# A fused long-convolution and MLP layer on one core: the planner's order replaced by a written-out order, PSUM buffers named one by one, some small steps free to move between VectorE and GpSimd

## The chip, the cores and the metric

One core of one Trainium2 chip. The metric is device time in microseconds (us) of one launch. The kernel before took 324.35, 325.56 and 326.74 us in three runs; the median is 325.56. Engines: PE = TensorE, DVE = VectorE, ACT = ScalarE, POOL = GpSimd, SP = SyncE, which here only issues DMAs.

## What is computed

The reference, cut to what matters (S = 2048 positions, D = 640 channels, F = 1728, all tensors bf16):

```python
mod = (silu(c) @ w_mod).reshape(1, 6, 1, 640)          # six vectors of 640: sa, ca, ga, sb, cb, gb
sa, ca, ga, sb, cb, gb = mod[:, 0], mod[:, 1], ...
h = layernorm(A_q) * (1 + ca) + sa
k_shift[s] = sum over t < 4 of k_pad[s + t] * shift_k[:, 3 - t]       # per channel
kv = k_shift * A_v
y  = irfft(rfft(kv padded to 4096) * rfft(ssm_k padded to 4096))[:2048] + kv * ssm_D
x  = A_q + ga * (h * y)
h  = layernorm(x) * (1 + cb) + sb
# the mixer on h:
m1 = gelu(layernorm(h) @ w1)              # its four channel groups are then shifted by +1, -1, +2, -2 positions
x1 = h + shifted(m1) @ w2
x  = x + gb * (x1 + gelu(layernorm(x1) @ w3) @ w4)
```

## The kernel before, in words

The convolution is a Fourier transform written as matmuls in two stages. `stage1` (PE line 472, 20 units of 4 matmuls) transforms 128-position blocks that DVE has transposed into place (`to_slots`, line 459) with the small table `F1bd`; `stage2` (PE line 490, 32 units of 4 matmuls) applies the table `Gs`. Both write PSUM, and `evac` (lines 271 to 277) copies each unit to SBUF, on ACT (line 274) or on DVE (line 276). The pair runs twice: first for the filter `ssm_k`, then for kv. Before the second time `k_shift` (PE line 523, 10 units of 8 matmuls with diagonal weights built by POOL at line 421) makes the shifted k and DVE multiplies it by v (line 528). The tables come from POOL index patterns, range reductions on DVE (lines 360/361) or on POOL (`angles_pool`, lines 374 to 376, three instructions of 512 elements each), sines on ACT, and DMAs that copy table halves (lines 419/420). Also ahead of the transform, POOL adds `ssm_D` to the first column of each of the five filter blocks (line 507), and the DVE transpose of the block comes after that.

The six modulation vectors (`mods`) are made in 12 halves. Each half loads 400 KB of `w_mod` into one of three buffers (SP, line 543), multiplies on PE (5 matmuls, line 549), and is added to or copied from PSUM.

`inverse1` (10 steps, lines 639 to 666) copies a spectrum with its two partition halves exchanged (two DMAs at line 645, one issued by SP and one by POOL, into four buffers in turn), makes two products on DVE (line 649), 32 matmuls on PE (lines 660/661) and two evictions on ACT. `inverse2` (6 steps, PE line 699, evictions on ACT) gives y. Then, in 8 groups of two 128-row tiles: `chain_a` (lines 751 to 765: DVE lines 756 and 759, ACT sum of squares line 748), `chain_b`, `chain_c`, each ended by `ln_finish` (lines 729 to 745: six tiny POOL instructions of 128x2 elements, in two halves 734 to 736 and 741 to 743); `turn` transposes the result (PE line 789 for groups 0 to 2, DMA transposes on SP line 782 for others); `mm_w1` (PE 836/846), `mm_w2` (PE 891, DVE 899), `mm_w3` (PE 924), `mm_w4` (PE 942/948, DVE 965/970/971, output DMAs 974). The last tile of all is ended by `last_tile` (lines 976 to 993): PE makes its two halves of 320 columns one after the other, and each half has its own two DVE instructions (986, 989) and output DMAs (992).

`ln1_stats` (lines 583 to 590: two BN_STATS and one BN_AGGR per tile) and `make_q` (lines 629 to 634: one normalization and two DVE products per tile) prepare layernorm(A_q).

What sets the order: every step is a task with an engine (or two to choose from), a modelled cost, and the regions that it reads and writes. `Planner.run` places the tasks by list scheduling over these costs. Ties go by RANK, a list with one number for each of the 1047 tasks. The instructions are issued in that order on each engine. PSUM is a ring of four buffers of two banks each, handed out in rotation: the fifth allocation waits until the first is empty.

## Time and profile before

| | us |
|---|---|
| median of the runs (lowest, highest) | 325.56 (324.35, 326.74) |
| span of the profiled execution, first to last instruction | 327.8 |
| PE busy | 278.0 (85%) |
| DVE busy | 218.0 (66%) |
| ACT busy | 199.7 (61%) |
| POOL busy | 122.7 (37%) |
| chain of waits that ends last: PE 56%, DVE 17%, POOL 8%, DMA 6%, ACT 5%, issue 5% | |

The profiled execution's own time is its span, 327.8 us; it lies 2.2 us above the median of the runs. Lines of the form "L649" name lines of the kernel. "Idle before, releaser" means that the engine stood still before that instruction, and what ended the wait. "PEclk" is TensorE's granted clock, 1.00 being the full 2.4 GHz and 0.50 being 1.2 GHz.

### The profile page before, as it was taken

Reading aid. Unit: us, or ns where it says so; the run is one execution under the profiler, and the core shown is the slowest. Engines: PE = TensorE matmul, PEld = TensorE weight load, DVE = VectorE, ACT = ScalarE, POOL = GpSimd, SP = SyncE. Lnnn points to the kernel's source line nnn. Section 1 sums busy time; section 2 is a strip of 40 time slices with the busy share of each in tenths; the row PEclk is TensorE's granted clock in tenths of the full one; section 3 lists DMA queues with packets and bytes.
Section 4 is the critical chain, followed back from the end, with each engine's and each line's share of the span. In section 5 each row is a group of like instructions: output and inputs, shape, how many; then the busy total and the mean of one; then the engine's idle time right before and its main releaser. Section 6 shows DMA issues by size and latency. Waiting matters only on the chain.

```text
span 327.8 us, 7133 instructions
## 1 busy us (share of the span) xinstructions
PE 278.0 (85%) x2816; PEld 205.8 (63%) x2816; DVE 218.0 (66%) x422; ACT 199.7 (61%) x314; POOL 122.7 (37%) x268
## 2 busy tenths in 40 slices
PE   0689998897958864376899899999999999999992
PEld 0455445664558762254588688788878688778761
DVE  6978999987989999879788899641140532440152
ACT  3586469787937867988888889546606245004300
POOL 8998600215062158656666567420200112000000
PEclk9979999999968995559899999999999999999998
DMA  6999999979676530094010130342310003210011
GB/s 235 225 240 204 225 244 206 219 206 255 160 190 174 125 102 9 15 338 196 3 29 14 21 81 20 73 92 40 18 44 22 20 23 61 48 36 20 0 43 40
DMA packets 56690, 35.39 MB, mean 108 GB/s; under 512 B 38528, under 2 KB 53504, under 8 KB 56656
## 3 DMA queue, kind: packets, MB, share of 16 engines
q1 hardware_dynamic: 55248, 30.63, 39.6%
q0 software_dynamic: 1312, 4.26, 5.0%
q8 instruction: 22, 0.36, 0.5%
q14 instruction: 12, 0.10, 0.1%
q10 hardware_dynamic: 96, 0.04, 0.1%
HBM read 16.31 MB, written 2.62 MB: 58 GB/s over the span
## 4 chain that ended last, share of the span: by engine, by line
PE 56%; DVE 17%; POOL 8%; DMA 6%; ACT 5%; issue 5%; SPq 0%; DVEq 0%; POOLq 0%; ACTq 0%
PE ps_w L924 16%; PE ps_w L942 14%; PE ps_ksh L523 6%; PE ps_w L891 5%; PE ps_w L836 5%; DVE R L276 4%; DVE Rb L649 4%; DMA RH<-in_w_mod_dram 3%; PE ps_s L472 3%; ACT RG L748 2%; DVE ln_st L588 2%; POOL lnv L742 2%; DMA RK<-in_w_mod_dram 2%; PE ps_s L490 2%; PE ps_mod L549 1%
## 5 line engine op out<-in xcount | busy, mean ns | idle before, releaser
L924 PE MATMUL ps_w<-R,T 128*128 128x256 bf16 x560 | 63.6, 273 | 0.0
L924 PEld LDWEIGHTS <-T 128*128 128x128 bf16 x560 | 54.8, 98 | 6.9
L942 PE MATMUL ps_w<-T,R 128*128 128x320 bf16 x416 | 59.0, 299 | 0.0
L928 ACT ACTIVATE R<-ps_w 128x1024 bf16<-128x1024 f32 (+1 forms) x32 | 29.3, 915 | 42.5 <-PE ps_w L924 42.2
L942 PEld LDWEIGHTS <-R 128*128 128x128 bf16 x416 | 40.2, 98 | 16.5 <-issue 1.6
L965 DVE TENSOR_TENSOR T<-ps_w,R 128x640 bf16<-128x640 f32 x15 | 12.4, 824 | 53.7 <-PE ps_w L948 43.4
L274 ACT CAST T<-ps_s 128x1024 bf16<-128x1024 f32 x32 | 30.9, 1024 | 13.2 <-PE ps_s L472 13.1
L472 PE MATMUL ps_s<-F1bd,Rb 128*128 128x256 bf16 x160 | 22.7, 293 | 11.6 <-DVE Rb L459 10.1
L748 ACT ACTIVATE RG<-R 128x640 bf16<-128x640 bf16 x32 | 23.6, 736 | 14.1 <-DVE R L899 14.0
L274 ACT CAST R<-ps_s 128x640 bf16<-128x640 f32 x42 | 27.5, 734 | 4.0 <-PE ps_s L490 3.8
L891 PE MATMUL ps_w<-RG,R 128*128 128x320 bf16 x160 | 25.6, 312 | 3.8 <-ACT R L852 2.3
L472 PEld LDWEIGHTS <-Rb 128*128 128x128 bf16 x160 | 16.8, 106 | 16.9 <-DVE Rb L459 10.2
L660 PE MATMUL ps_i<-EA,Rb 128*128 128x128 bf16 x160 | 21.6, 236 | 5.3 <-DVE Rb L649 5.3
L274 ACT CAST T<-ps_i 128x1024 bf16<-128x1024 f32 x20 | 19.4, 1015 | 9.1 <-issue 4.7
L490 PE MATMUL ps_s<-T,RG 64*128 64x320 bf16 x256 | 23.1, 297 | 1.7 <-ACT R L274 1.0
L899 DVE SCALAR_TENSOR_TENSOR R<-ps_w,R 128x640 bf16<-128x640 f32 x16 | 13.1, 821 | 15.7 <-PE ps_w L891 15.7
L734 POOL TENSOR_SCALAR lnv<-stat 128x2 f32<-128x2 f32 x24 | 6.5, 272 | 45.2 <-DVE R L899 37.1
L891 PEld LDWEIGHTS <-R 128*128 128x128 bf16 x160 | 15.8, 102 | 11.4 <-ACT R L852 3.0
L836 PE MATMUL ps_w<-R,RG 128*128 128x256 bf16 x160 | 20.9, 291 | 2.1 <-DVE R L797 2.0
L661 PE MATMUL ps_i<-EB,Rb 128*128 128x128 bf16 x160 | 21.6, 236 | 0.8 <-DVE Rb L649 0.8
L742 POOL TENSOR_TENSOR lnv<-lnv,mhalf 128x2 f32<-128x2 f32 x24 | 20.5, 856 | 1.9
L660 PEld LDWEIGHTS <-Rb 128*128 128x128 bf16 x160 | 17.0, 107 | 6.3 <-DVE Rb L649 6.3
(151 smaller groups left out, 517.5 us busy)
## 6 DMA issues: line engine op xcount, KB each, us to landing
RH<-in_w_mod_dram SPq DMA_DIRECT2D x8, 400.0 KB, 5.2
Ra<-in_A_ssm_k_dram SPq DMA_DIRECT2D x5, 512.0 KB, 5.8
Ra<-in_A_q_dram SPq DMA_DIRECT2D x8, 320.0 KB, 9.1
out_dram<-RH SPq DMA_DIRECT2D x60, 40.0 KB, 1.6
T<-in_B_w_dram SPq DMA_DIRECT2D x1, 2160.0 KB, 13.4
T<-in_B_w_dram SPq DMA_DIRECT2D x1, 2080.0 KB, 10.0
RK<-in_w_mod_dram SPq DMA_DIRECT2D x4, 400.0 KB, 6.5
RK<-R POOLq DMA_DIRECT2D x5, 256.0 KB, 4.0
```

Of the source, the lines that this page charges most:

```text
L274: nc.scalar.copy(dst, src(ps.tile))
L472: nc.tensor.matmul(psv[:, ml, :], lhsT=xL[:, s0:s0 + P], rhs=F1r, start=True, stop=True)
L490: nc.tensor.matmul(psv[:, g], lhsT=Gs[p, k, 64 - 64 * cc:192 - 64 * cc], rhs=T1b[p, cc * 32 + k], start=(cc == 0), stop=(cc == 1), tile_po ...
L660: nc.tensor.matmul(psv[:, w, :], lhsT=Av[:, r_, :, g_], rhs=EAf, start=True, stop=False)
L661: nc.tensor.matmul(psv[:, w, :], lhsT=Bv[:, r_, :, g_], rhs=EBf, start=False, stop=True)
L742: nc.gpsimd.tensor_tensor(rs, rs, mhalf[:, 0:n], ALU.pow)
L748: add("ACT", 0.74, lambda e: nc.scalar.activation(junk, src, ACT.Square, scale=float(D) ** -0.5, accum_out=stat[:, li, 1, t:t + 1]), r=[sk ...
L836: nc.tensor.matmul(pt[:, fb, :], lhsT=w1_sb[:, b, 160 * fb:160 * fb + P], rhs=hT[:, b, :], start=(b == 0), stop=(b == ND - 1))
L891: nc.tensor.matmul(pt[:, hf, 0:320], lhsT=gsf[:, fb, c0:c0 + P], rhs=w2_sb[:, fb, 320 * hf:320 * hf + 320], start=(fb == 0), stop=(fb == 4))
L924: nc.tensor.matmul(pt[:, fl, :], lhsT=w3_sb[:, b, fb * P:(fb + 1) * P], rhs=xT[:, b, :], start=(b == 0), stop=(b == ND - 1))
L928: nc.scalar.activation(g3[g % 2][:, f0:f0 + fn, :], ps.tile[:, 0:fn, :], ACT.Gelu_apprx_tanh)
L942: nc.tensor.matmul(pts[i][:, hf, 0:320], lhsT=gg[:, fb, i * P:(i + 1) * P], rhs=w4_sb[:, fb, 320 * hf:320 * hf + 320], start=(fb == 0 and ...
```

## The change

RANK and the list scheduling are gone. ORDER is a written list of all 1055 tasks; a word such as `90P:0` says "task 90, on PE, in PSUM buffer 0". There are four PSUM buffers as before, but each has its own tag, so a task takes the buffer that the word names and not the next in rotation. Tasks that may run on two engines have the engine in the word too.

Of the steps that the change lets run on POOL or DVE, ORDER leaves all 12 pieces of `angles_pool` and the table E on POOL, and moves to DVE one of the two negations of `Gs`, one of the five `ssm_D` additions and 12 of the 24 first halves of `ln_finish`. Of the 20 `inverse1` evictions the last two go to DVE; the 12 of `inverse2` stay on ACT. In the last `mm_w4` the two column halves of the last tile lie in two PSUM buffers, not one.

```diff
-RANK = """
-6 8 9 11 12 13 14 15 17 18 19 21 22 24 25 26 27 29 381 86 103 20 16 49 638 369 93 684 23 109 168 254 105 161 91 81 540 69 391 68 60 28 378 34 373 71
...
+ORDER = """
+19G 0S 18D 20D 21G 23D 22D 24A 56G 27G 29D 28D 25A 2S 31A 30A 36G 37G 68G 69D 26G 90P:0 91A 86P:1 6S 87A 88P:2 89A 4S 72G 73D 104P:3 105A 102P:0
...
     def run(self):
-        engs = ("PE", "ACT", "DVE", "POOL", "SP")
...
+        order, seen = [], set()
+        for word in ORDER.split():
+            head, _, places = word.partition(":")
+            t = self.tasks[int(head[:-1])]
+            t.on = self.CODE[head[-1]]
+            for sl, place in zip(t.alloc, places):
+                sl.place = place
...
-    psA = ctx.enter_context(tc.tile_pool(name="psA", bufs=4, space=PSUM))
+    psA = ctx.enter_context(tc.tile_pool(name="psA", bufs=1, space=PSUM))
...
-            ps.tile = psA.tile(shape or [P, 2, 512], dt, name=name, tag="q2")
+            ps.tile = psA.tile(shape or [P, 2, 512], dt, name=name, tag="q" + ps.place)
...
-                nc.gpsimd.tensor_scalar(xs, ti, s_col, off, ALU.mult, ALU.add)
-                nc.gpsimd.tensor_scalar(xr, xs, MAGIC, MAGIC, ALU.add, ALU.subtract)
-                nc.gpsimd.tensor_tensor(xs, xs, xr, ALU.subtract)
...
+            add(both, {...}, lambda e, off=off: eng_of[e].tensor_scalar(xs, ti, s_col, off, ALU.mult, ALU.add), ...)
+            add(both, {...}, lambda e: eng_of[e].tensor_scalar(xr, xs, MAGIC, MAGIC, ALU.add, ALU.subtract), ...)
+            add(both, {...}, lambda e: eng_of[e].tensor_tensor(xs, xs, xr, ALU.subtract), ...)
...
     for b in range(ND):
-        add("POOL", 0.25, lambda e, b=b: nc.gpsimd.tensor_tensor(sT[:, b, 0:1], sT[:, b, 0:1], Dcol[:, b:b + 1], ALU.add),
+        add(("POOL", "DVE"), {...}, lambda e, b=b: eng_of[e].tensor_tensor(sT[:, b, 0:1], sT[:, b, 0:1], Dcol[:, b:b + 1], ALU.add),
...
     def ln_finish(li, t0, n):
         def f(e):
-            nc.gpsimd.tensor_scalar(nm, s1, -1.0 / D, None, ALU.mult)
-            nc.gpsimd.tensor_tensor(rs, nm, nm, ALU.mult)
-            nc.gpsimd.tensor_scalar(rs, rs, -1.0, EPS, ALU.mult, ALU.add)
+            eng_of[e].tensor_scalar(nm, s1, -1.0 / D, None, ALU.mult)
+            eng_of[e].tensor_tensor(rs, nm, nm, ALU.mult)
+            eng_of[e].tensor_scalar(rs, rs, -1.0, EPS, ALU.mult, ALU.add)
...
     def mm_w4(g):
-        pss = (Slot(), Slot())
+        pss = tuple(Slot() for _ in range(3 if g == 7 else 2))
...
+                tl = [pst(s, name="ps_w4") for s in pss] if i == 0 else [s.tile for s in pss]
+                pts = [[tl[0], tl[0]], [tl[1], tl[-1]]]
...
-            t1 = add("DVE", 0.48, lambda e, c=c, hf=hf: nc.vector.tensor_tensor(bo[:, c], ps.tile[:, hf, 0:320], gbv[:, c], ALU.mult),
+            t1 = add("DVE", 0.48, lambda e, c=c, hf=hf: nc.vector.tensor_tensor(bo[:, c], pss[hf].tile[:, hf, 0:320], gbv[:, c], ALU.mult),
```

POOL at the start of the program. Before (the `ssm_D` additions are line 507, Ra holds the filter blocks, R_67 is scratch for table angles, F1bd is the table of `stage1`):

```order
L374 TENSOR_SCALAR R_67<-R_67,s64t,offc 128x512
L375 TENSOR_SCALAR R_67<-R_67 128x512
L376 TENSOR_TENSOR R_67<-R_67 128x512
L507 TENSOR_TENSOR Ra<-Ra,Dcol 128x1 x3
L398 AFFINE_SELECT F1bd<-F1c 128x256
L399 AFFINE_SELECT F1bd<-F1bd 128x256
L507 TENSOR_TENSOR Ra<-Ra,Dcol 128x1
L374 TENSOR_SCALAR R_67<-R_67,s64t,offc 128x512
```

After (the same steps are lines 307, 309, 311 for the angles, 440 for the additions, 333/334 for F1bd):

```order
L307 TENSOR_SCALAR R_67<-R_67,s64t,offc 128x512
L440 TENSOR_TENSOR Ra<-Ra,Dcol 128x1
L333 AFFINE_SELECT F1bd<-F1c 128x256
L334 AFFINE_SELECT F1bd<-F1bd 128x256
L440 TENSOR_TENSOR Ra<-Ra,Dcol 128x1
L309 TENSOR_SCALAR R_67<-R_67 128x512
L311 TENSOR_TENSOR R_67<-R_67 128x512
L440 TENSOR_TENSOR Ra<-Ra,Dcol 128x1
```

The first addition and the `stage1` table now stand ahead of two of the three angle instructions; before, they stood behind all three.

SP, the loads of the front. Before (line 301 is a DMA transpose of a k or v block, 576 a quarter of half of A_q, 543 a half of a modulation weight, 645 an `inverse1` copy; above these rows stand eight more transposes):

```order
L301 DMA_TRANSPOSE R_68<-in_A_k_dram 128x2048
L301 DMA_TRANSPOSE R_68<-in_A_v_dram 128x2048
L576 DMA Ra<-in_A_q_dram 32x8x640 x4
L543 DMA RK<-in_w_mod_dram 128x5x320
L543 DMA RH<-in_w_mod_dram 128x5x320
L576 DMA Ra<-in_A_q_dram 32x8x640 x4
L543 DMA RH<-in_w_mod_dram 128x5x320 x2
L645 DMA RG<-R_67 64x2048
L543 DMA RH<-in_w_mod_dram 128x5x320
L543 DMA RK<-in_w_mod_dram 128x5x320
```

After (lines 234, 509, 476 for these; 354 and 355 are the table copies, all six of which POOL issued before; above these rows stand three transposes, of k, v and k):

```order
L234 DMA_TRANSPOSE R_68<-in_A_v_dram 128x2048
L354 DMA RG<-RG 64x1536
L225 DMA c_col<-in_c_dram 128x5x1
L509 DMA Ra<-in_A_q_dram 32x8x640
L354 DMA RG<-RG 64x1536 x2
L355 DMA RG<-RG 64x1536
L476 DMA RH<-in_w_mod_dram 128x5x320
L355 DMA RG<-RG 64x1536
L509 DMA Ra<-in_A_q_dram 32x8x640 x3
L476 DMA RH<-in_w_mod_dram 128x5x320
L234 DMA_TRANSPOSE R_68<-in_A_k_dram 128x2048
```

The table copies, half of A_q and the first two modulation loads now stand between the second and the third pair of k and v transposes.

DVE where `inverse1` ends and `chain_a` begins. Before (649 is an `inverse1` product, 588/589 are `ln1_stats`, 756/759 `chain_a`, 633/634 and 626 `make_q`; six more pairs of 588/589 stand between the first two rows):

```order
L649 TENSOR_TENSOR Rb<-R_68,R_67 128x4x8x64
...
L588 BN_STATS ln_st<-Ra 128x6 x2
L589 BN_AGGR mv_96<-ln_st 128x2
L756 TENSOR_TENSOR R_68<-Rb,RQ 128x8x5x16 x2
L759 SCALAR_TENSOR_TENSOR Ra,stat<-R_68,Ra 128x640 x2
L633 TENSOR_TENSOR RQ<-RQ,modv 128x640
```

After (582 the product, 210 an eviction from PSUM, 566/567 `make_q`, 521/522 `ln1_stats`; two more pairs of 521/522 stand between the last two rows):

```order
L582 TENSOR_TENSOR Rb<-R_68,RK 128x4x8x64
L210 CAST T_66<-ps_i_1463 128x128x8
L210 CAST T_66<-ps_i_1486 128x128x8
L567 TENSOR_TENSOR RQ<-RQ,modv 128x640 x2
L566 TENSOR_TENSOR RQ<-RQ,modv 128x640
L567 TENSOR_TENSOR RQ<-RQ,modv 128x640
L521 BN_STATS ln_st<-Ra 128x6 x2
L522 BN_AGGR mv_96<-ln_st 128x2
...
L689 TENSOR_TENSOR R_68<-Rb,RQ 128x8x5x16
```

Between the last product and `chain_a` stand three `ln1_stats` where there were seven, and two evictions and four `make_q` products that stood elsewhere. Before the first product, DVE now has two `make_q` normalizations, two products of line 633, five of line 634 and one `stage1` eviction less than before, and one negation and one addition more; three of the `make_q` products stand between the first `inverse1` products.

Three more moves are told in words. On PE, 7 of the 10 `k_shift` units stood ahead of the filter's `stage2` and 3 among its first units; now 4 stand ahead of it and 6 among the `stage1` units of kv. Of the 12 modulation units 11 stood behind the filter's `stage2` and ahead of kv's, and one after 3 of its 32 units; now 2 stand at the end of the filter's `stage2`, 4 among kv's `stage1`, and 6 are spread over kv's `stage2`, the last one behind its last unit. Of the 10 pairs of `inverse1` copies four stood ahead of the first product before, and one does after; the last three quarters of the second half of A_q are loaded after the copies. And the first `mm_w4` stands later in PE's order: behind 6 tiles of `mm_w2` and 120 matmuls of `mm_w3`, where it stood behind 4 tiles and 70.

## Rows read from the trace of the kernel before

**Rows 1.** By stretch: length, busy PE, PEld, DVE, ACT, POOL, PEclk, DMA share, GB/s
```profile
8.00:92.00 84.00, 72.32 (x556) 42.82 (x556) 75.17 (x101) 62.82 (x86) 37.35 (x58) 0.98 0.98 215
...
123.00:142.00 19.00, 7.83 (x371) 4.83 (x351) 17.34 (x46) 17.33 (x31) 14.06 (x31) 0.52 0.18 50
142.00:190.00 48.00, 42.25 (x327) 31.80 (x328) 39.62 (x100) 40.06 (x79) 28.75 (x68) 0.90 0.28 90
190.00:322.00 132.00, 131.50 (x1092) 103.79 (x1092) 50.58 (x107) 56.00 (x93) 23.22 (x70) 1.00 0.19 40
```
**Rows 2.** Timeline of PE (start us, length, instructions; idle before and its releaser)
```profile
10.07 5.03 PE L472 MATMUL ps_s<-F1bd,Rb 128*128 128x256 bf16 x24 [10.07 <-DVE Rb L459]
...
142.14 4.43 PE L836 MATMUL ps_w<-R,RG 128*128 128x256 bf16 x20 [1.26 <-DVE R L797]
...
154.87 3.89 PE L891 MATMUL ps_w<-RG,R 128*128 128x320 bf16 x16 [2.28 <-ACT R L852]
...
160.09 2.36 PE L836 MATMUL ps_w<-R,RG 128*128 128x256 bf16 x20 [0.77 <-DVE R L797]
...
317.79 3.71 PE L942 MATMUL ps_w<-T,R 128*128 128x320 bf16 x26
```
**Rows 3.** Timeline of DVE, six places
```profile
7.96 10.02 DVE L459 STREAM_TRANSPOSE Rb<-Ra 128x1024 int32<-128x1024 int32 x5 [1.44 <-POOL Ra L507]
...
91.61 1.21 DVE L649 TENSOR_TENSOR Rb<-R,RG 128x2048 bf16<-128x2048 bf16 x1
...
116.55 0.87 DVE L588 BATCH_NORM_STATS2 ln_st<-Ra 128x6 f32<-128x320 bf16 x2
...
123.55 0.84 DVE L756 TENSOR_TENSOR R<-Rb,RQ 128x640 bf16<-128x640 bf16 x2
...
321.53 0.49 DVE L986 TENSOR_TENSOR T<-ps_w,modv 128x320 bf16<-128x320 f32 x1 [1.76 <-PE ps_w L942]
...
322.30 0.48 DVE L986 TENSOR_TENSOR T<-ps_w,modv 128x320 bf16<-128x320 f32 x1
```
**Rows 4.** Timeline of POOL: the start, and the first ln_finish
```profile
6.32 1.31 POOL L376 TENSOR_TENSOR R<-R 128x512 f32<-128x512 f32 x1
7.60 0.33 POOL L507 TENSOR_TENSOR Ra<-Ra,Dcol 128x1 bf16<-128x1 bf16 x2
...
127.09 0.43 POOL L734 TENSOR_SCALAR lnv<-stat 128x2 f32<-128x2 f32 x1
...
128.47 0.32 POOL L741 TENSOR_TENSOR lnv<-stat,lnv 128x2 f32<-128x2 f32 x1
...
130.31 0.22 POOL L734 TENSOR_SCALAR lnv<-stat 128x2 f32<-128x2 f32 x1
```
**Rows 5.** The chain of waits, 57 to 79 us (start us, us, what)
```profile
57.35 5.48 DMA RH<-in_w_mod_dram
...
63.76 5.01 DMA RH<-in_w_mod_dram
...
73.24 5.69 DMA RK<-in_w_mod_dram
```
**Rows 6.** DVE groups by line (count, busy us, mean ns, idle before)
```profile
L276 DVE CAST T<-ps_s 128x1024 bf16<-128x1024 f32 x8 | 9.4, 1211 | 0.4 <-PE ps_s L472 0.4
...
L633 DVE TENSOR_TENSOR RQ<-RQ,modv 128x640 bf16<-128x640 bf16 x16 | 7.7, 483 | 0.0
L346 DVE TENSOR_SCALAR offc<-offc 128x1 f32<-128x1 f32 x1 | 0.1, 143 | 0.0
```
**Rows 7.** DMA issues, 91 to 118 us (KB each, median us to landing)
```profile
RK<-R POOLq DMA_DIRECT2D x3, 256.0 KB, 4.2
```
**Rows 8.** Timeline of SP (an issue's length includes its wait)
```profile
34.90 3.12 SPq L301 DMA_TRANSPOSE R<-in_A_v_dram  x1
...
47.62 10.11 SPq L543 DMA_DIRECT2D RH<-in_w_mod_dram  x2
...
323.70 1.82 SPq L992 DMA_DIRECT2D out_dram<-RH  x4
```

More of the change, by code (lines that the diff above doesn't have):

```diff
@@ L55 @@
+1001S 1028P:2 1029A 1030P:0 985D 989S 926S 1024P:1 1031A 987S 1010P:32 986S 988S 979D 983S 980S 1026P:0 925S 927S 1012D 1025A 928S 1013D 1016S 1011P
+1018D 982S 1014S 981S 1019D 1021S 1020S 1023S 1027A 1032P:130 1022S 1035D 1036D 1017S 1015S 1040S 1037S 1033P 1043D 1039S 1044D 1048S 1047S 1038S
+1045S 1034P 1049D 1050D 1053S 1052A 1046S 1051S 1054A
 """
 class Task:
-    __slots__ = ("no", "eng", "cost", "fn", "deps", "prio", "lat", "alloc", "frees", "left", "succ", "start", "end", "on", "ready", "kb", "rate", "port")
+    __slots__ = ("no", "eng", "cost", "fn", "deps", "lat", "alloc", "frees", "succ", "on", "kb", "rate", "port", "act")
@@ L123, in run @@
     def run(self):
-        engs = ("PE", "ACT", "DVE", "POOL", "SP")
-        free = dict.fromkeys(engs, 0.0)
-        ready = {e: [] for e in engs}
-        slots = []
-        order = []
-        wire = 0.0
-        held = {"DVE": 0.0, "POOL": 0.0}
-        rank = RANK.split()
-        if rank:
-            for t in self.tasks:
-                t.prio = (int(rank[t.no]), t.no)
-        def cost(t, e):
-            return t.cost[e] if isinstance(t.cost, dict) else t.cost
-        def push(t):
-            for e in (t.eng if isinstance(t.eng, tuple) else (t.eng,)):
-                ready[e].append(t)
@@ L218 @@
     small = ctx.enter_context(tc.tile_pool(name="small", bufs=2))
-    psA = ctx.enter_context(tc.tile_pool(name="psA", bufs=4, space=PSUM))
+    psA = ctx.enter_context(tc.tile_pool(name="psA", bufs=1, space=PSUM))
     pl = Planner(4)
     add = pl.add
-    eng_of = {"ACT": nc.scalar, "DVE": nc.vector}
+    eng_of = {"ACT": nc.scalar, "DVE": nc.vector, "POOL": nc.gpsimd}
     Ra = mem.tile([P, 10240], BF, name="Ra")
@@ L266, in cd, with dma, evac @@
         return 0.14 + 0.00104 * n
-    def dma(eng, kb, fn, r=(), w=(), prio=None, rate=330.0):
-        return add(eng, {"SP": 0.5, "POOL": 0.6}, lambda e: fn(nc.sync if e == "SP" else nc.gpsimd), r, w, prio, kb=kb, rate=rate)
-    def evac(dst, src, n, ps, w, prio=None, eng=("ACT", "DVE")):
+    def dma(eng, kb, fn, r=(), w=(), rate=330.0):
+        return add(eng, {"SP": 0.5, "POOL": 0.6}, lambda e: fn(nc.sync if e == "SP" else nc.gpsimd), r, w, kb=kb, rate=rate)
+    def evac(dst, src, n, ps, w, eng=("ACT", "DVE")):
         def f(e):
@@ L1004 @@
            lambda q: q.dma_start(w4_sb[64:128, NF - 1, :], B_w4[(NF - 1) * P:F, :])]
[L1005 to L1006 removed]
+    dma("SP", 2200, w3t[0], w=[("T01", 0, ND * FP)])
+    dma("SP", 2200, w3t[1], w=[("T01", 10240, 10240 + NF * D, "w4")])
     for i in (2, 3):
[L1008 removed]
+        dma("SP", 100, w3t[i], w=[("T01", 10240, 10240 + NF * D, "w4")])
     def f(e):
         nc.gpsimd.tensor_copy(w3_sb[:, :, F:FP], w3_sb[:, :, F - 64:F])
[L1012 removed]
+    add("POOL", 0.6, f, w=[("T01", 0, ND * FP)])
     made = 5
     for g in range(8):
[L1015 to L1018 removed]
+        ra = chain_a(g)
+        rb = chain_b(g, ra)
+        chain_c(g, rb)
         while made < NT and made <= 2 * g + 6:
[L1020 removed]
+            make_q(made)
             made += 1
[L1022 removed]
+        mm_w1(g)
         if g >= 1:
[L1024 removed]
+            mm_w2(g - 1)
         if g >= 2:
[L1026 to L1028 removed]
+            mm_w3(g - 2)
+            mm_w4(g - 2)
+    mm_w2(7)
     for g in (6, 7):
[L1030 to L1031 removed]
+        mm_w3(g)
+        mm_w4(g)
     order = pl.run()
[L1034 to L1038 removed]
     with tc.manual_schedule():
```

461 lines of the change are left out of this document (207 added, 254 removed), and 27 rows, old and new, of the table RANK.

## The prediction

> **What bounds the kernel now.** I read the busy time by stretch first, because one share for the whole run hides that the kernel has two halves. From 190 to 322 us PE is busy for 131.50 of 132 us at full clock [rows 1]: nothing that only reorders can shorten that part, and the matmuls are the same in number. Everything that can be won lies before 190 us and after 322. From 8 to 92 us PE is busy for 72.32 of 84, ACT for 62.82, but DVE for 75.17: DVE is the nearest to a bound, with 8.83 us idle. From 123 to 142 us PE works for 7.83 of 19 us at a granted clock of 0.52 while DVE and ACT each work for 17.3: this is the chain of small layernorm steps that feeds the first `mm_w1`. From 142 to 190 PE is busy for 42.25 of 48, 5.75 idle.
>
> Then the timelines, for the events that each stretch hands on. DVE starts its first transpose at 7.96 us after 1.44 us of waiting for POOL [rows 3], and PE's first matmul waits for DVE until 10.07 [rows 2]. The first `inverse1` product starts at 91.61, the seven `ln1_stats` behind the last product at 116.55, `chain_a` at 123.55 [rows 3], the first `mm_w1` at 142.14 [rows 2]. PE ends at 317.79 + 3.71 = 321.50, and DVE's last steps only then begin [rows 2, 3]; the span ends at 327.8. So the forecast is a sum of how much earlier each of these events comes.
>
> **The change part by part.** All terms are made against the profiled span, 327.8 us.
>
> *Start.* POOL reaches the first `ssm_D` addition at 7.60 because an angle instruction stands ahead of it until 6.32 + 1.31 = 7.63 [rows 4]. The addition now stands two angle instructions earlier, so the wait of 1.44 us goes [rows 3]; DVE is busy with its own angles until 6.5, and that is late next. Gain 1.4. Least 0.8, if the first filter block lands later than the addition could run.
>
> *Front, from there to the first product.* Three things. (a) DVE work that now stands behind the first product: two normalizations and two products of `make_q` and five more of its products, nine instructions at about 0.48, and one `stage1` eviction at 1.21 [rows 6], 5.5 us; one negation and one addition come in, about 0.5 (I price them by the 128x640 product, 0.48, from above and by the tiny 0.143 from below [rows 6]). Net 5.0. (b) Of DVE's 8.83 us of idle [rows 1], 1.44 is counted under the start; 7.4 is left. The chain of waits shows what much of it hangs on: three loads of a modulation weight, 5.48, 5.01 and 5.69 us [rows 5], stand one behind the other in the chain between 57 and 79, because the matmul of one half frees the buffer for a later load and all these matmuls stand together. The new order spreads the twelve halves from the filter's `stage2` to the end of kv's, so a load of 5.5 us has other PE work over it. Nothing in the rows says that all idle goes; I take half, 3.7, with the ends at 0 and 7.4. (c) Against it, three `make_q` products now stand between the `inverse1` products: 3 x 0.48 = 1.4. Together 5.0 + 3.7 - 1.4 = 7.3.
>
> *Between the products and `chain_a`.* Seven `ln1_stats` filled 123.55 - 116.55 = 7.0 us, 1.0 each [rows 3]. Now two evictions at 1.21, four products at 0.48 and three `ln1_stats` stand there: 2.4 + 1.9 + 3.0 = 7.3. Loss 0.3. The evictions may move out of ACT's way the end of the last one, but `chain_a` is behind them on DVE either way; ends -1 and +1. The four `ln1_stats` that left go to the stretches behind, 4 us of DVE work beside matmuls.
>
> *`chain_a` to the first `mm_w1`*: 142.14 - 123.55 = 18.6 us [rows 2, 3], of which DVE and ACT each fill over 90% [rows 1]. The first half of an `ln_finish` took POOL from 127.09 to 128.47, 1.4 us with three instructions [rows 4]; on DVE three tiny instructions cost at least 3 x 0.143 = 0.43 [rows 6], I take 0.5. Two such steps stand in series ahead of the first `mm_w1`, so 2 x 0.9 = 1.8, and 0.7 more for `make_q` work that no longer stands in the chain's way. Gain 2.5; ends 0.6 (the second half waits for ACT's sum of squares anyway) and 4. The twelve moved halves are 12 x 0.5 = 6 us more for DVE; it had 48 - 39.62 = 8.4 idle between 142 and 190 and 81 after [rows 1], which covers them.
>
> The Trainium skill bears on this term ("Perfetto Trace Analysis", section "Optimizing Scalar/DVE Operations"): GpSimd and DVE share an SBUF read port, so moving work between these two might not help. The trace fits it in so far as the same tiny instruction took POOL 0.43 us at 127.09 and 0.22 at 130.31 [rows 4]; whether the port did that, no row shows. By that rule alone the term would be its lower end, 0.6, and the sum 1.9 us later, still inside the forecast's range.
>
> *First `mm_w1` to saturation.* PE loses 5.75 us of idle here, and 4.43 - 2.36 = 2.1 us by the half clock of the first `mm_w1` [rows 1, 2]. The largest single wait, 2.28 us for ACT before an `mm_w2` [rows 2], stands in the new order behind a second and a third `mm_w1`. I take 2.0, with ends -2 (DVE has 6 us of new halves and 4 of `ln1_stats` here) and +4.
>
> *End.* Both halves of the last tile were one PSUM tile, and DVE's first multiplication waited until 321.53 though half of the 26 matmuls were done at about 317.79 + 3.71 / 2 = 319.65 [rows 2, 3]. With two buffers the second half's multiplication is the one that waits, and starts at 321.53 instead of 322.30: 0.77. SP's last four output issues took 1.82 us [rows 8], and the two of the first half now go out before PE ends: 0.9 more. Gain 1.7; ends 0.8 and 1.9.
>
> Naming buffers freely, without a rotation, costs no instruction; where it removes a wait, that is part of the terms above.
>
> **Sum**: 1.4 + 7.3 - 0.3 + 2.5 + 2.0 + 1.7 = 14.6 us; 327.8 - 14.6 = 313.2 us for a profiled execution. The profile lay 2.2 above the median of the runs, so 311.0 us in the runs, 4.5% less than 325.56.
>
> **The rivals.**
>
> *The front gives nothing.* SP waits inside an issue: two modulation loads took SP 10.11 us at 47.62, because the second waited for its buffer [rows 8], and everything behind stood still. In the new order table copies, which need POOL's and ACT's tables, stand on SP ahead of six of the ten k and v transposes, which feed `k_shift` and so DVE. If they hold SP until 30 us (my assumption, a quarter into the front; no row shows the new wait), six transposes of 3.1 us end near 49, where the last ended at 38.0 before [rows 8], and kv is late. For it: POOL, which makes these tables, was busy for 37.35 us between 8 and 92 [rows 1]. Against it: before, the modulation loads that stand among kv's `stage1` were waited for only from 57.35 on [rows 5], so 49 need not be late. If it holds, 7.3 becomes 0 and the sum is 7.3 us: 318.3 in the runs.
> The Trainium skill states the same of the issuing side ("DMA: Bandwidth & Descriptors", section "Anatomy of one DMA — SWDGE (gpsimd) path"): a DMA's semaphore wait happens on the issuing sequencer before dispatch. The row of 10.11 us agrees.
>
> *No change to speak of.* PE's clock. From 123 to 142 it was granted 0.52 after sparse work [rows 1], and the first `mm_w1` ran at 4.43 instead of 2.36 [rows 2]. If the new order leaves such gaps that the next matmuls stay at half clock as well, each 10 us of full-clock work take 10 more; with that, the 2.0 lost and the front at half its gain the sum is 14.6 - 10 - 2.0 - 3.6 = -1.0: 326.6 in the runs. For it: the half clock stands in the row. Against it: the clock came back by 160 with the gaps that it had [rows 2].
>
> *Slower: `inverse1` starves on its copies.* Before, four of ten pairs of copies had been issued ahead of the first product; now one. A pair is 2 x 256 KB, POOL's half lands 4.2 us after its issue [rows 7], and the ten steps took (116.55 - 91.61) / 10 = 2.5 us each [rows 3]. It starts to decide once a pair takes more than 2.5 us. At 215 GB/s, the rate of the front [rows 1], a pair needs 2.4 us of wire, and with four buffers in turn three pairs can be under way: nothing is lost. If each waits instead until the step before has freed its buffer, nine steps take 4.2 each: 9 x 1.7 = 15 us. The three quarters of A_q behind the copies on SP, and the `ln1_stats` that read them, then come late as well, by some 4 us. 327.8 - 14.6 + 19 = 332.2, 330.0 in the runs. Against it: four buffers.
>
> **How the numbers follow.** A measurement of this kernel can tell a change of about 1% (3.3 us) from none. Forecast 0.62; the front gives nothing 0.20; no change to speak of 0.11; starving 0.07. Faster by over 1% are the first two and a little less of each, 0.81; within 1% 0.11; slower 0.08. The ends of the terms: if all gains are at their upper ends, 1.4 + 10.9 + 0.7 + 4 + 4 + 1.9 = 23 us, 302.7; not all will be, so the low end is 304.5. At the high side the range reaches over the first rival to 321.5; the second and the third lie outside.
>
> **What would show it.** Right: the first DVE transpose before 7 us; no modulation load of 5 us in the chain between 57 and 79; the first product at 83 to 86; `chain_a` at about 115; the first `mm_w1` at about 130; PE full for the same 131 us; the last but one multiplication of 128x320 starting about 2 us before PE ends. Wrong: a first product later than 90, waits of DVE on copies between products, a granted clock at 0.5 beyond 20 us after the first `mm_w1`, or SP standing in a table copy beyond 30 us.

## The result, and the profile after

The changed kernel took 314.55 us (median of four runs, 312.59 to 315.64). The kernel before had a fourth run, of 333.17 us, which counts as one of the chip's slow state and is left out, so its median stays 325.56 us. The ratio is 0.965, with a 95% interval of 0.958 to 0.972. That is 3.5% faster. The forecast was 311.0 us, 4.5% faster; the time lies inside the range.

The profiled execution of after spans 311.9 us, 15.9 less than the 327.8 of before, while the medians of the runs differ by 11.0. The two profiles overstate the gain by some 5 us. The run that the profile of after shows took 313.61 us, so a run is 1.7 us longer than its span. By that, the profiled execution of before belongs to a run of about 329.5, 3.9 above its median, and that of after lies 0.9 below its own. The terms below are told between these two profiles.

Windows of the kernel before, cut at its first DVE transpose, first product and `chain_a` (columns as in [rows 1]):

```profile
7.96:91.61 83.65, 72.32 (x556) 42.82 (x556) 74.81 (x100) 62.86 (x86) 37.13 (x57) 0.98 0.98 216
91.61:123.55 31.94, 24.68 (x548) 23.10 (x551) 29.64 (x43) 20.65 (x22) 13.12 (x29) 0.89 0.56 150
```

The same stretches after, then 57 to 82 and the stretches that answer to the rest of [rows 1]:

```profile
6.26:79.80 73.54, 68.87 (x556) 41.98 (x556) 70.98 (x93) 62.97 (x88) 35.70 (x54) 1.00 1.00 224
79.80:111.73 31.93, 24.34 (x471) 22.27 (x473) 31.06 (x39) 20.15 (x23) 8.24 (x15) 0.89 0.86 212
...
57.00:82.00 25.00, 22.21 (x214) 13.55 (x211) 23.79 (x37) 21.71 (x32) 6.00 (x12) 0.99 0.91 213
...
113.00:130.00 17.00, 8.72 (x302) 5.67 (x291) 16.03 (x45) 15.02 (x29) 11.29 (x31) 0.50 0.26 80
130.00:176.00 46.00, 41.09 (x337) 32.33 (x336) 35.84 (x97) 33.01 (x66) 21.16 (x54) 0.94 0.29 93
176.00:306.00 130.00, 129.90 (x1070) 100.83 (x1069) 67.23 (x157) 63.02 (x108) 22.34 (x64) 1.00 0.20 42
```

The reader is to see where 11.8 us went. Up to the first product the stretch shrank by 10.1 us. DVE's work there fell by 74.81 - 70.98 = 3.83 us, its idle time from 83.65 - 74.81 = 8.84 to 73.54 - 70.98 = 2.56. DVE now works for 97% of it. The first transpose came 1.70 us earlier: 3.83 + 6.28 + 1.70 = 11.8. From the first product to `chain_a` nothing changed in length: 1.4 us more DVE work went into idle time. Behind 176 PE is as full as it was.

Who ended the waits in the front of before tells where the idle time lay (its view of waits: who waited for whom, us in total, times, longest):

```profile
DVE R L528 <- PE ps_ksh L523: 4.5, 4, 2.1
...
PE ps_mod L549 <- DMA RH<-in_w_mod_dram: 3.3, 5, 1.1
```

DVE waited longest for `k_shift` products (4.5 us, in four waits between 19 and 43 us), ahead of the modulations. PE waited 3.3 us for modulation loads into RH, and 0.9 for one into RK. In after DVE has no wait for `k_shift` and PE none for a modulation load. Up to 57 us DVE's idle time fell from 4.85 to 1.36 us, from there to the first product from 3.99 to 1.21.

DVE's timeline after (answers to [rows 3]):

```profile
6.26 2.07 DVE L394 STREAM_TRANSPOSE Rb<-Ra 128x1024 int32<-128x1024 int32 x1 [0.39 <-POOL Ra L440]
...
79.80 1.22 DVE L582 TENSOR_TENSOR Rb<-R,R 128x2048 bf16<-128x2048 bf16 x1
...
111.73 0.44 DVE L689 TENSOR_TENSOR R<-Rb,RQ 128x640 bf16<-128x640 bf16 x1
...
117.52 0.17 DVE L667 TENSOR_SCALAR lnv<-stat 128x2 f32<-128x2 f32 x1
...
305.22 0.49 DVE L920 TENSOR_TENSOR T<-ps_w,modv 128x320 bf16<-128x320 f32 x1
...
306.99 0.49 DVE L920 TENSOR_TENSOR T<-ps_w,modv 128x320 bf16<-128x320 f32 x1 [0.91 <-PE ps_w L876]
```

PE's timeline after ([rows 2]):

```profile
128.12 1.23 PE L779 MATMUL ps_w1x<-R,RG 128*128 128x256 bf16 x5 [0.68 <-DVE R L730]
129.13 4.00 PE L769 MATMUL ps_w<-R,RG 128*128 128x256 bf16 x20
...
145.39 2.35 PE L769 MATMUL ps_w<-R,RG 128*128 128x256 bf16 x20
...
303.25 3.71 PE L876 MATMUL ps_w<-T,R 128*128 128x320 bf16 x26
```

The first `mm_w1` came 14.0 us earlier, still mostly at half clock (a granted clock of 0.50 from 113 to 130 us; 4.00 us for 20 matmuls, the third such group 2.35). PE ends at 306.96, 14.5 us earlier, and the first half of the last tile (305.22) no longer waits for that end. Of the three modulation loads of [rows 5] one is left in the chain of waits:

```profile
69.27 0.79 PE ps_mod L482 x5
70.05 0.03 PE ps_s L424
70.08 4.93 DMA RH<-in_w_mod_dram
```

SP's timeline after ([rows 8]; L354 and L355 are the copies of table halves, L926 the last outputs):

```profile
23.16 1.12 SPq L354 DMA_DIRECT2D RG<-RG  x2
24.39 0.53 SPq L355 DMA_DIRECT2D RG<-RG  x1
...
29.19 0.46 SPq L355 DMA_DIRECT2D RG<-RG  x1
...
31.84 6.34 SPq L234 DMA_TRANSPOSE R<-in_A_k_dram  x1
...
48.81 3.10 SPq L234 DMA_TRANSPOSE R<-in_A_v_dram  x1
...
307.94 1.83 SPq L926 DMA_DIRECT2D out_dram<-RH  x4
```

SP holds the last six k and v transposes behind the table copies and is through with them at 51.9 us; before it was at 38.0. That is the wait that the first rival spoke of, and the rows show no cost of it: from 30 to 57 us PE is busy for 26.77 of 27, DVE for 26.23.

### The profile page after: what moved, and what is told of

Same layout as the page of the kernel before. It is cut to its first block, busy times and chain, and to the rows that moved or that the text cites. A ratio compares the mean times of both kernels' runs of the same rounds, so it can differ in the third digit from the quotient of the medians.

```text
span 311.9 us, 7129 instructions
## 1 busy us (share of the span) xinstructions
PE 275.1 (88%) x2816; PEld 204.7 (66%) x2816; DVE 228.1 (73%) x460; ACT 197.3 (63%) x314; POOL 101.8 (33%) x227
## 4 chain that ended last, share of the span: by engine, by line
PE 59%; DVE 19%; ACT 8%; POOL 4%; issue 4%; DMA 3%; SPq 0%; DVEq 0%; ACTq 0%; POOLq 0%
PE ps_w L876 18%; PE ps_w L857 17%; PE ps_w L824 5%; DVE Rb L582 5%; PE ps_w L769 4%; PE ps_ksh L456 4%; ACT R L208 3%; PE ps_s L407 2%; PE ps_s L424 2%; DMA Ra<-in_A_ssm_k_dram 2%; PE ps_mod L482 2%; DMA RH<-in_w_mod_dram 2%; DVE R L704 2%; DVE Rb L394 2%; DVE R L461 1%
## 5 line engine op out<-in xcount | busy, mean ns | idle before, releaser
L861 ACT ACTIVATE R<-ps_w 128x1024 bf16<-128x1024 f32 (+1 forms) x32 | 28.5, 910 | 26.9 <-PE ps_w L857 26.9
L208 ACT CAST T<-ps_s 128x1024 bf16<-128x1024 f32 x33 | 31.8, 1018 | 7.4 <-PE ps_s L407 7.2
L208 ACT CAST R<-ps_s 128x640 bf16<-128x640 f32 x42 | 26.8, 724 | 2.7 <-PE ps_s L424 2.4
L824 PE MATMUL ps_w<-RG,R 128*128 128x320 bf16 x160 | 23.4, 299 | 1.5 <-ACT R L771 1.4
L674 POOL TENSOR_TENSOR lnv<-stat,lnv 128x2 f32<-128x2 f32 x24 | 7.0, 290 | 51.7 <-ACT RG L681 44.9
L208 ACT CAST T<-ps_i 128x1024 bf16<-128x1024 f32 x18 | 17.2, 1026 | 9.1 <-PE ps_i L594 8.4
L424 PE MATMUL ps_s<-T,RG 64*128 64x320 bf16 x256 | 21.8, 297 | 0.8 <-ACT R L208 0.3
L769 PE MATMUL ps_w<-R,RG 128*128 128x256 bf16 x160 | 21.7, 299 | 0.0
L675 POOL TENSOR_TENSOR lnv<-lnv,mhalf 128x2 f32<-128x2 f32 x24 | 19.4, 810 | 1.9
L769 PEld LDWEIGHTS <-RG 128*128 128x128 bf16 x160 | 17.2, 108 | 3.7 <-issue 0.3
```

The source lines that it names most:

```text
L208: nc.scalar.copy(dst, src(ps.tile))
L424: nc.tensor.matmul(psv[:, g], lhsT=Gs[p, k, 64 - 64 * cc:192 - 64 * cc], rhs=T1b[p, cc * 32 + k], start=(cc == 0), stop=(cc == 1), tile_po ...
L675: nc.gpsimd.tensor_tensor(rs, rs, mhalf[:, 0:n], ALU.pow)
L769: nc.tensor.matmul(pt[:, fb, :], lhsT=w1_sb[:, b, 160 * fb:160 * fb + P], rhs=hT[:, b, :], start=(b == 0), stop=(b == ND - 1))
L824: nc.tensor.matmul(pt[:, hf, 0:320], lhsT=gsf[:, fb, c0:c0 + P], rhs=w2_sb[:, fb, 320 * hf:320 * hf + 320], start=(fb == 0), stop=(fb == 4))
L861: nc.scalar.activation(g3[g % 2][:, f0:f0 + fn, :], ps.tile[:, 0:fn, :], ACT.Gelu_apprx_tanh)
```

## The experiments

All start from the changed kernel, except "Only the modulations spread" and "The kernel before, once more". In these kernels a word names a task, its engine and buffers, as in the change. Where their front is that of after, the first product starts between 79.6 and 81.5 us in single executions, so differences of up to 2 us at that place mean nothing in one profile. From there to `chain_a` it takes 31.0 to 32.8 us in eight kernels in which that stretch has the order of after. Behind that, intervals repeat better: `chain_a` to the first `mm_w1` takes 16.38 or 16.39 us in eight executions, the first `mm_w1` to PE's end 178.7 to 180.0 in eight. The runs resolve less: the interval of after's ratio, 0.958 to 0.972, overlaps that of every kernel below that lies within 4 us of it, so there the reading rests on the intervals of one profile.

**Modulations together.** Nine of the twelve halves stand among the last kv `stage1` and the first kv `stage2` units again, their loads with them (238P is a half's matmuls, 239D its addition, 246S a load).

```diff
-132P:3 312P:2 313A 135D 133D 238P:0 239D 292P:1 293A 314P:3 315A 316P:2 287D 243S 244P:0 245D 240S 318P:1
+132P:3 312P:2 238P:0 239D 246S 313A 135D 133D 292P:1 293A 314P:3 241P:0 242D 249S 315A 316P:2 244P:0 245D 252S 287D 318P:1
```

> The changed kernel with 9 of the 12 modulation units put back together on PE, among the last ten stage1 units of kv and the first three of its stage2, and their loads on SP moved with them. Theory (the loads in series were what held the front, and spreading them took idle time away): three rounds of 5 to 6 us loads stand between about 57 and 75 us again, the first product comes 4 to 6 us later than 79.8, at 84 to 86, and all of it reaches the end: 317 to 320 us in the runs. Rival (the front is faster because DVE has less to do and SP's loads are placed better, the modulation was only the wait that showed): first product within 1.5 us of 79.8, end within 1.5 us of the changed kernel.

Measured: 334.48 us, ratio to before 1.026 (1.018 to 1.034). The first product starts at 101.51 us, 21.7 later than in after. The chain of waits of this kernel:

```profile
53.67 7.59 DMA RK<-in_w_mod_dram
...
70.07 3.67 DMA RH<-in_w_mod_dram
...
74.67 3.60 DMA RH<-in_w_mod_dram
...
81.44 4.71 DMA RK<-in_w_mod_dram
```

Its window from 57 to 82 us, to be held against that of after above:

```profile
57.00:82.00 25.00, 14.01 (x80) 8.60 (x80) 9.73 (x13) 6.40 (x7) 2.06 (x5) 0.80 0.55 139
```

The mechanism is the one named: the loads are back in the chain, and DVE works for 9.73 of 25 us where it worked for 23.79. The price was four to five times the expected one. In the new SP order the third and later loads are issued from 52 us on, behind the last transpose, where before issued its third at 47.6; that this is the reason was not tested. So the run shows that the new SP order needs the spread, not what the spread brought: the kernel is slower than before.

**Only the modulations spread, on the kernel before.** The planner's order is written out word for word, and ten of the twelve halves are spread as after has them (230P, 233P: the matmuls of two halves; 238S, 241S: loads; numbers are those of before).

```diff
-384S 385G 293A 230P 202D 235S 296P 228A 238S 294P 231D 297A
+384S 385G 293A 202D 235S 296P 228A 294P 297A
...
+306P 230P 238S 231D 290P 307A 312P 233P 241S 234D
```

> The kernel before with one part of the change alone: the modulation units spread on PE as in the new order (2 behind the filter's stage2, 4 among kv's stage1, 6 over kv's stage2), their evictions and the loads that wait for their buffers moved with them; everything else, with the ring of PSUM buffers, as before. Theory (the loads in series take DVE's and PE's time in the front): first inverse1 product 3 to 5 us earlier than 91.6, at 86.5 to 88.5, and the end 3 to 5 us earlier than the kernel before. Rival (spreading helps only with the new SP order, where the k and v blocks and the tables come at other times): first product within 1.5 us of 91.6.

Measured: 336.36 us, ratio 1.030 (1.025 to 1.035): slower by 10 us. The theory fell. The first product starts at 96.16 instead of 91.61, and then DVE works for only 7.49 of 13 us between 92 and 105. The chain there:

```profile
91.05 0.14 SPq L551
...
94.41 2.00 DMA RH<-RK
...
96.62 0.50 SPq L587
...
99.36 12.48 DMA RG<-R
```

Line 551 is nine copies into RH, where the modulation weights lay: they wait for the last half. The `inverse1` copies (L587) stand behind them on SP, and the one issued at 99.36 then takes 12.48 us, right behind the load of the mixer's weights (L617, issued at 98.20). This is the starving that the slower rival described, by another cause: the place of the copies on SP. Spreading alone moves a wait; the change also gives the copies their places. The first product itself was late ahead of these copies; what held it was not taken apart.

**Table copies on POOL.** Five copies leave SP, so that nothing holds the transposes.

```diff
-34S
+34G
...
-47S 46S
+47G 46G
...
-35S
+35G
...
-48S
+48G
```

> The changed kernel with the five table copies that SP issues given back to POOL, so that SP no longer stands behind the tables; nothing else moved. Theory (DVE is full in the front, so earlier k and v blocks find nobody free): SP's last k and v transpose issued some 5 to 10 us before 52, first product within 1 us of 79.8, end within 1 us of the changed kernel. Rival from the prediction (SP held behind the tables delays kv): first product 2 to 4 us earlier. Other side (five more issues of 0.6 us on POOL delay its own tables): first product 1 to 3 us later.

Measured: 324.65 us, ratio 0.994 (0.991 to 0.997); the first product at 89.84, 10.0 us later. Every expectation missed. SP's timeline:

```profile
26.06 10.80 SPq L234 DMA_TRANSPOSE R<-in_A_k_dram  x1
...
47.94 3.19 SPq L234 DMA_TRANSPOSE R<-in_A_v_dram  x1
```

the chain of waits:

```profile
32.91 8.22 DMA RG<-RG
...
41.18 3.91 PE ps_s L424 x27
```

and the filter's `stage2` in the groups of PE:

```profile
L424 PE MATMUL ps_s<-T,RG 64*128 64x320 bf16 x256 | 25.2, 340 | 7.2 <-DMA RG<-RG 6.3
```

The transposes were issued 6 us earlier and were through at 51.1 instead of 51.9. The last table copy was issued late by POOL and then took 8.22 us; in after the five copies of 192 KB that SP issues land in a median of 4.3. The filter's `stage2` starts at 28.05, as in after (28.32), but stands for 6.3 us in three waits for table copies, the last until 41.18; in after it waits for none.

**Table copies on POOL, at once.** To tell the late issue from the slow copy, the copies go out as soon as their halves are made.

```diff
-43G 34S 7S
+43G 34G 7S
...
-203S 45G 47S 46S 78P:1 79D 35S 82P:2
+203S 45G 47G 46G 48G 78P:1 79D 35G 82P:2
...
-195A 199D 234S 48S 202S
+195A 199D 234S 202S
```

> As the run with the table copies on POOL, but with the last of them ahead of the tables E and the silu steps on POOL. Theory (the copy crawls because the k and v transposes, no longer held behind it, fill the DMA engines at the same time): the copy still takes 6 us or more to land, the filter's stage2 still stands, first product at 84 to 87. Rival (the copy was only late in POOL's queue): first product within 1.5 us of 79.8.

Measured: 326.9 us, ratio 0.999 (0.995 to 1.003); the first product at 92.92. The chain:

```profile
23.31 8.09 DMA RG<-RG
...
32.45 9.63 DMA RG<-RG
```

Issued at 23.31, the last of the four copies of line 354 took 8.09 us, and those that need them (line 355, issued once they had landed) 9.63 more. So the lateness is not POOL's other work alone: the copies are slow. The theory had that right and the place wrong (92.92 for 84 to 87), and its reason, the transposes, does not hold as it stands. SP's timeline of this kernel:

```profile
23.32 1.66 SPq L509 DMA_DIRECT2D Ra<-in_A_q_dram  x3
...
25.65 11.21 SPq L234 DMA_TRANSPOSE R<-in_A_k_dram  x1
```

From 23.3 to 31.4 us only 85 of 1533 DMA packets are under 512 B, the size that transposes move (2330 of 2362 in before from 29.7 to 33.3, among transposes). So the copy of 8.09 us lay beside loads of A_q and of modulation weights, which SP issues there because no table copy stands ahead of them. And in before POOL issued all six copies, between 19.27 and 37.99, while SP issued transposes until 38.0:

```profile
RG<-RG POOLq DMA_DIRECT2D x6, 192.0 KB, 4.4
```

They landed in 3.4 to 6.1 us. So neither the transposes nor POOL's queue makes a copy slow by itself. The loads are the rival that is left; no run moved them alone, and the cause stays open. The Trainium skill states that DMAs of all issuing engines run on the same 16 DMA engines and interleave ("DMA: Bandwidth & Descriptors", section "Issuing engines are not separate DMA queues"); a copy of POOL's that is slow beside loads of SP's fits that, but how the 16 engines shared the time was not looked into.

**The four `ln1_stats` back ahead of `chain_a`.**

```diff
-204S 220D 226D 219D 519D 520D
+204S 220D 226D 219D 225D 223D 222D 229D 519D 520D
```

> The changed kernel with four ln1_stats put back between the inverse1 products and chain_a on DVE, so that seven stand there as before. Theory (DVE is the path there and what is moved behind lies beside matmuls): chain_a 4.0 us later, at 115.7, first mm_w1 3 to 4 us later, end 3 to 4 us later, 317.5 to 318.5 in the runs. Rival (the moved work only costs again later, in the chain between chain_a and the full PE): chain_a 4.0 later, but PE's end less than 1.5 us later.

Measured: 318.29 us, ratio 0.978 (0.971 to 0.986). From the first product to `chain_a` 35.07 us instead of 31.93 (+3.1 for 4 us of DVE work, 2.3 above the highest of the others), the first `mm_w1` at 131.05 (+2.9), PE's end at 310.90 (+3.9). The theory held: this work costs nearly its length there, and little behind.

**Two angle instructions first again, on POOL.**

```diff
-36G 37G 68G
+36G 37G 38G 39G 68G
...
-107A 38G 39G 40A
+107A 40A
```

> The changed kernel with the second and third angle instruction on POOL put back ahead of the first ssm_D addition. Theory: first DVE transpose at 7.9 instead of 6.3, and the front, where DVE is full, hands all 1.6 us on: first product at 81.4, end 1.6 us later. Rival: an idle stretch of DVE further on takes it up, first product within 0.5 us of 79.8.

Measured: 315.51 us, ratio 0.970 (0.961 to 0.978). The first transpose starts at 7.53 instead of 6.26, and PE ends 2.2 us later in its profile; the runs differ from after's by 1.0, inside their scatter. The theory held at the first transpose; how much of that the runs keep isn't resolved.

**The twelve `ln_finish` halves back on POOL.**

```diff
-558D 560D 475S
+558D 560G 475S
...
-533D 535D 511P:10
+533D 535G 511P:10
...
```

> The changed kernel with all 12 moved first halves of ln_finish back on POOL, in the same places of the order. Theory of the prediction: each is 0.9 us shorter on DVE, but only one of them (chain_b of group 0) stands ahead of the first mm_w1 in the new order, so the first mm_w1 comes 0.9 us later and the end 1 to 2 us later. Rival (the port that the two engines share or ACT's sum of squares decides, so the engine makes no difference): first mm_w1 and end within 0.5 us. Other side (DVE is the fuller engine, 12 x 0.5 us less work for it): end 0.5 to 2 us earlier.

Measured: 317.62 us, ratio 0.974 (0.968 to 0.981): 3.1 us slower than after. `chain_a` to the first `mm_w1` takes 17.26 instead of 16.39 us (+0.9), from there to PE's end 181.30 instead of 178.84 (+2.5, and 1.3 over the highest of the eight others). POOL's timeline of this kernel shows the first of the halves that moved:

```profile
119.50 0.41 POOL L667 TENSOR_SCALAR lnv<-stat 128x2 f32<-128x2 f32 x1
120.00 0.25 POOL L668 TENSOR_TENSOR lnv<-lnv 128x2 f32<-128x2 f32 x1
120.33 1.07 POOL L669 TENSOR_SCALAR lnv<-lnv 128x2 f32<-128x2 f32 x1
```

From the first start to the last end that is 1.90 us. On DVE in after such an instruction takes 0.17 us (117.52 above), and the three end 0.57 us after their start. So the halves on DVE do help here, by this profile more behind the first `mm_w1` than ahead of it. The Trainium skill's caution about the shared read port ("Perfetto Trace Analysis", section "Optimizing Scalar/DVE Operations") did not decide this case.

**One PSUM buffer for the last tile.**

```diff
-        pss = tuple(Slot() for _ in range(3 if g == 7 else 2))
+        pss = tuple(Slot() for _ in range(2))
...
-                last_tile(t, pss[1:], t0, tl)
+                last_tile(t, (pss[1], pss[1]), t0, tl)
```

> The changed kernel with both halves of the last tile in one PSUM buffer again. Theory: the first half's multiplication waits for PE's end, so from PE's end to the end of the span it takes 6.3 us as before and not 4.9; 1.4 us more, and nothing earlier moves. Rival (the queue of output issues on SP decides, and it is full either way): less than 0.5 us.

Measured: 314.67 us, ratio 0.963 (0.958 to 0.968). From the start of the last 26 matmuls to the span's end 8.79 us, against 8.65 in after and 10.01 in before. PE's timeline:

```profile
305.11 1.94 PE L876 MATMUL ps_w<-T,R 128*128 128x320 bf16 x13
307.63 1.93 PE L876 MATMUL ps_w<-T,R 128*128 128x320 bf16 x13 [0.58 <-DVE T L920]
```

The theory missed: the first half's multiplication (at 307.09) did not wait for PE's end. With one buffer PE itself waits, because the reader of the first half is listed ahead of the second half's matmuls. That order is not the one that before had, so one more kernel lists the reader behind them:

```diff
-1033P 1043D 1039S 1044D 1048S 1047S 1038S 1045S 1034P 1049D
+1033P 1039S 1038S 1034P 1043D 1044D 1048S 1047S 1045S 1049D
```

> One PSUM buffer for both halves of the last tile, as in the earlier run, and the first half's two DVE steps listed behind the second half's matmuls, as the kernel before lists them. Theory (a wait on a PSUM tile goes by what is listed before it, so one buffer costs only if the reader is listed late): the first multiplication starts after PE's end, and from the start of the last 26 matmuls to the end of the span it takes 10.0 us as before, not 8.7. Rival (SP's queue of issues decides): 9.0 or less.

Measured: 314.79 us, ratio 0.966 (0.958 to 0.973). The first multiplication waits for PE's end, as in before:

```profile
306.59 0.49 DVE L920 TENSOR_TENSOR T<-ps_w,modv 128x320 bf16<-128x320 f32 x1 [1.76 <-PE ps_w L876]
```

The end takes 312.2 - 302.85 = 9.35 us, between the theory's and the rival's figures. So the late reader is worth 0.7 us of the 1.36 gained, and what else differs at the end the other 0.7; that this is SP's queue alone was not shown. The runs can't resolve either.

**Buffers in rotation.** Each allocation takes the next of the four buffers again. Where the rotation would lock, tasks move (51 places).

```diff
-116P:0 110P:2 119D 84P:3
+116P:0 119D 110P:1 84P:2
```

> The changed kernel with the PSUM buffers in rotation again: each allocation takes the next buffer of the four, and a task stands later in the list where that buffer is not yet released in it. Engines as in the new order. Theory (freely named buffers only spare a few waits; the order of steps is what gains): 0 to 2 us slower than the changed kernel. Rival (naming buffers is what lets the front be full on DVE): first product 3 us or more later than 79.8.

Measured: 354.23 us, ratio 1.085 (1.080 to 1.090). The first product comes at 82.40, so at least 9 of the front's 11.8 us don't hang on free buffers. The interval from there to `chain_a` grows by 5.9 us, and from the first `mm_w1` to PE's end by 30. Groups of PE from 138 us on:

```profile
L857 PE MATMUL ps_w<-R,T 128*128 128x256 bf16 x560 | 66.5, 279 | 12.8 <-DVE T L899 7.7 <-ACT R L861 4.7 <-ACT R L728 0.4
...
L769 PE MATMUL ps_w<-R,RG 128*128 128x256 bf16 x160 | 20.4, 287 | 9.7 <-ACT Rb L208 7.0 <-DMA R<-RK 2.7
```

In after the first of these groups has 0.5 us of idle in the whole run. Neither expectation held: the kernel is 40 us slower than after, not 0 to 2, and most of the loss lies behind the first product, which is 2.6 us later. The written order can't be had with a rotation, as it names buffers that happen to be free; so the run changes buffers and order together, and what the names alone are worth is not shown.

**The kernel before, once more.** No edit.

> The kernel before, unchanged, for a second profile. The runs of the changed kernel are 1.7 us longer than their spans; the profiled span of before, 327.8, would then belong to a run of 329.5, which is 3 us above the median of before. Theory: a second profile has a span of 323 to 326, and the difference lies in the front, where loads land at other times. Rival: 327 to 329 again, and profiled executions of before are simply longer.

Measured: 327.08 us, span 325.4. The span is as the theory had it, but the place is not: the first product starts at 92.56, later than the 91.61 of the first profile. From there to `chain_a` it takes 30.76 us for 31.94, and from the first `mm_w1` to PE's end 177.2 us, where the first profile has 179.4. DVE's waits for `k_shift` come again, 5.1 us in five.

**A try at better.** Three `ln1_stats` move behind `chain_b` of the first group, and the outputs of the last two tiles are issued by SP and ACT in turn.

```diff
-204S 220D 226D 219D 519D 520D
+204S 519D 520D
...
-503A 531D 527D 532D 528D 504A 529D 530A 561G 533D 535D 511P:10
+503A 531D 527D 532D 528D 504A 529D 530A 561G 533D 535D 220D 226D 219D 511P:10
...
-                qe = ("SP", "ACT")[cg % 2] if hf else "SP"
+                qe = ("SP", "ACT")[cg % 2]
```

> A version meant to beat both: the changed kernel with the last three ln1_stats moved from between the inverse1 products and chain_a to behind chain_b of group 0 on DVE, and with every second output issue of the last two tiles on ACT's queue instead of SP's. Theory (DVE alone sets chain_a; four ln1_stats put back cost 3 to 4 us): the evictions of the first inverse2 end at 109.8, so chain_a comes 1.8 us earlier, at 109.9, and the first matmul of mm_w1 1.8 earlier, at 126.3; from PE's end to the end of the span 0.8 to 1.2 us less than 4.9. Together 2 to 3 us: 311.5 to 312.5 in the runs. Rival (the three only move their cost to the chain of groups 1 and 2): less than 1 us together.

Measured: 314.86 us, ratio 0.963 (0.956 to 0.969): no gain. `chain_a` follows the first product 1.4 us sooner (30.49 for 31.93, but only 0.5 below the lowest of the others; ACT is late there next, by 1.08). DVE's timeline:

```profile
123.25 0.89 DVE L521 BATCH_NORM_STATS2 ln_st<-Ra 128x6 f32<-128x320 bf16 x2
...
126.16 0.21 DVE L522 BATCH_NORM_AGGREGATE mv<-ln_st 128x2 f32<-128x12 f32 x1
```

They now stand ahead of the normalization that PE's transpose waits for, and `chain_a` to the first `mm_w1` takes 19.06 us instead of 16.39. The rival held: the cost only moved. At the end 314.0 - 309.92 = 4.1 us instead of 4.94, too little for the runs to show.

## Why the prediction was right, term by term

The last column holds after against the second profile of before (span 325.4).

| stretch | predicted gain, us | between the profiles, us | second profile of before, us |
|---|---|---|---|
| start | 1.4 | 1.70 | 1.70 |
| front (a): DVE work moved behind | 5.0 | 3.83 | 3.70 |
| front (b): DVE idle | 3.7 | 6.28 | 7.36 |
| front (c) and products to `chain_a` | -1.4 - 0.3 | 0.0 | -1.2 |
| `chain_a` to first `mm_w1` | 2.5 | 18.59 - 16.39 = 2.2 | 2.2 |
| first `mm_w1` to PE's end | 2.0 | 179.36 - 178.84 = 0.5 | 177.16 - 178.84 = -1.7 |
| end | 1.7 | 1.36 | 1.4 |
| sum | 14.6 | 15.9 | 13.5 |

- *Start.* Right. The wait of 1.44 us fell to 0.39; with the angles first again the transpose came 1.3 us later.
- *Front.* The gain came, but for (b) the mechanism was only half of it. "I take half, 3.7" was the weak step: 6.28 of DVE's 8.84 us went. The prediction hung much of this idle time on the modulation loads. By DVE's idle time, 2.8 us of the gain lie behind 57 us, where the modulations stand, and 3.5 ahead of it, where DVE waited for `k_shift`, which the prediction had no term for. That the move of six `k_shift` units into kv's `stage1` took that wait away is read from the rows; no run put them back. That step also subtracted the start's 1.44 us from the idle, though that wait ended at 7.96 and lay outside the window that begins at 8. (a) brought less than priced, as steps that stayed took longer in this profile: two range reductions 0.91 us each (line 294) for 0.34 (line 361). Putting the loads together again (+21.7 us at the first product) shows that this order needs them spread, not what the spread brought. And no part has this gain by itself: spreading alone on the kernel before lost 10 us, moving the table copies to POOL lost 10.0 at the first product. The parts are links of one order, and what undoing one costs is no measure of what it brought. "No modulation load of 5 us in the chain" was nearly right: one is left. The first product came at 79.80, ahead of the 83 to 86 that the prediction named as its sign.
- *Between.* (c) priced three products between the `inverse1` steps as lost time; between the two profiles they fit into idle time. Against the second profile of before the stretch is 1.2 us longer, so a loss of that size is not ruled out.
- *`chain_a` to `mm_w1`.* The size fits, the reason only in part. "Two such steps stand in series": ORDER leaves the first of the two on POOL. Undoing all twelve halves cost 0.9 us here, one step's worth by the prediction's own price, and 2.5 us behind, where the prediction counted the halves only as work for DVE. What gave the other 1.3 was not tried.
- *First `mm_w1` to saturation.* 0.5 is not a gain that can be told from none: before itself took 179.36 and 177.2 in two profiles. The 2.0 did not come. PE's idle time there hardly fell (4.9 us from 130 to 176, for 5.75 from 142 to 190), and the half clock lasted longer in this profile: the second group of 20 matmuls took 3.65 us, where before's took 2.34.
- *End.* Right to 0.3 us. The earlier reading of the first half was priced at 0.77 and measured 0.7. It hangs on where the reader is listed: one buffer with the reader listed first lost only 0.14 us.
- *From the profile to the runs.* This step failed most. The terms were read from one execution above its median, and "The profile lay 2.2 above the median of the runs" carried their sum over unchanged: 14.6 us off the span became 14.6 us off the median. That 2.2 also compares a span with runs; in runs the execution lay 3.9 above the median, and the profiled run of after lay 0.9 below its own. So 15.9 us between the two executions are 15.9 - 3.9 - 0.9 = 11.1 between the medians, which is the measured 325.56 - 314.55 = 11.0. The sum was 1.3 too small for the profiles and 3.6 too large for the runs; that is the miss of 314.55 - 311.0 = 3.55 us. The second profile of before shows where the first one had lost time: 2.2 us from the first `mm_w1` to PE's end and 1.2 from the first product to `chain_a`.
- *Luck.* That the sum comes within 1.3 us of the profiles is in part luck: the `k_shift` waits that nobody priced made up for the 2.0 that did not come behind the first `mm_w1`.
- *The rivals.* "The front gives nothing" had SP's wait right (the last table copy left SP at 29.65, for the 30 it assumed) and its effect wrong; in the kernels with the copies on POOL, which don't have this wait, the front was 10.0 and 13.1 us worse. The half clock did not last (2.35 us by 145). The starving rival did not come in after, but appeared in the kernel with only the modulations spread.
